# Gathering the selector matmuls of block 0 into two groups of four chunks

## Chip, cores, metric

The kernel runs on one core of a Trainium2 chip. The metric is the device time of one execution in microseconds (us). "Before" is the kernel as it was, "after" the changed one. Times were taken in rounds, several executions of each kernel on the same chip.

## The reference, cut to what matters

Two pairs of layers work on 2048 tokens of width 1024: LayerNorm and a dilated sliding-window attention (32 heads of 32, window 8, step 2), then LayerNorm and a gated feed-forward layer.

```python
def _A_ref(x, wqkv, wo):                       # attention, cut
    q, k, v = ...                              # x @ wqkv, split by heads
    off = jnp.arange(W) * dil                  # W, dil = 8, 2
    logits = jnp.einsum("bhsd,bhswd->bhsw", q, kg) * scale
    logits = jnp.where(mask[None, None, :, :], logits, -1e9)
    attn = _softmax(logits, axis=-1)
    o = jnp.einsum("bhsw,bhswd->bhsd", attn, vg)
    return o.transpose(...).reshape(B, S, D) @ wo
x = x + _A_ref(_layernorm(x), A_wqkv, A_wo)
x = x + _B_ref(_layernorm(x), B_W_gate, B_W_up, B_W_down)
# ... and the same two lines once more
```

The change touches `logits` for the first block of 512 tokens (block 0) of the first pair.

## The kernel before

The tokens go through in four blocks of 512, twice. For block 0 the scores are made in eight chunks c = 0 to 7. TensorE makes q_c and k_c (eight 128x512 matmuls each, called an acc group here), ScalarE casts each out of PSUM, and VectorE multiplies q_c with the eight shifted views of k_c into prod_c (128 partitions x 4096). A selector matmul then sums over the partitions that belong to one head. Its weights are only 128x32, so four stand side by side in the array, one for each quarter of the tokens. Each chunk needs eight of them.

```python
    def red_mm(n, prod, first, last):
        ...
        with pe_group():                 # keeps TensorE in this order
            for wh in range(2):
                for tq in range(TPB):
                    mm(st["L"][32 * tq:32 * tq + 32, WH * wh:WH * (wh + 1), :], lhsT=sel[:],
                       rhs=prod[:, WH * wh:WH * (wh + 1), tq * P:(tq + 1) * P],
                       start=first, stop=last, skip_group_check=True, tile_position=(0, 32 * tq))

    def prod_direct_steps(n):            # block 0 only
        prods = {}
        def mult(c):
            def f():
                prods[c] = work.tile([P, W, BLK], BF16, tag="t", name=f"prod_{c}")
                ...
        def red(c):
            def f():
                red_mm(n, prods.pop(c), c == 0, c == KC - 1)
            return f
        return [mult(c) for c in range(KC)], [red(c) for c in range(KC)]
```

The program is written as a list of events with a time each (in estimated us). They are sorted and emitted, and so the order of the instructions on each engine comes out of these numbers (`t_qk0` and `t_qk1` are where the q and k work of blocks 0 and 1 begins, `GRP` is 1.73, the time of one acc group):

```python
    GAP0 = 2.05
    ...
    spread(qk_steps(0, ln_a[0], "qk01"), t_qk0, GAP0)     # q_0 k_0 q_1 k_1 ... k_7
    mults, reds = prod_direct_steps(0)
    for c in range(KC):
        ev.append((t_qk0 + GAP0 * (2 * c + 2.0), mults[c]))
        if c < KC - 2:
            ev.append((t_qk0 + GAP0 * (2 * c + 4.5), reds[c]))
    ...
    ev.append((t_qk1 + 0.5 * GRP, reds[KC - 2]))
    ev.append((t_qk1 + 2.5 * GRP, reds[KC - 1]))
    ev.append((t_qk1 + 2.6 * GRP, lambda: softmax(0)))
    ln1(2, t_qk0 + 10.0, t_qk1 + 5.0, True, 4.5)          # LayerNorm of block 2, on ScalarE
    spread(qk_steps(1, ln_a[1], "qk01"), t_qk1, GRP)      # q_0 q_1 q_2 k_0 ... of block 1
```

`ln1` gives ScalarE two statistics passes for each of four tiles of 128 tokens, and later one apply for each; at the time in its third argument a DMA transposes the result.

## Time and profile before

| | before |
|---|---|
| time, median of 3 (range) | 1630.64 us (1630.27 to 1630.65) |
| TensorE busy | 1618.6 of 1628.4 us |
| chain of waits, share of TensorE | 95% |
| TensorE waiting for other engines | 3.3 us |
| stretch, first acc_q matmul of block 0 to first acc_k of block 1 | 63.04 - 24.69 = 38.35 us |

The stretch holds everything that the change touches on TensorE.

From the profile page of before, the span, the first line of busy times (us, share of the span, instructions) and the chain of waits by engine:

```profile
span 1628.4 us, 18703 instructions
...
PE 1618.6 (99%) x7589; PEld 782.2 (48%) x7638; DVE 1062.6 (65%) x926; ACT 506.1 (31%) x1050; POOL 255.7 (16%) x220
...
PE 95%; DVE 4%; issue 1%; DMA 0%; POOL 0%; DVEq 0%
```

From the waits view of before, for TensorE: waiting line, releaser, us in total, times, longest.

```profile
PE scratch L129 <- DVE ones L296: 1.5, 1, 1.5
PE dacc L129 <- DVE x L700: 0.8, 1, 0.8
PE acc_v L129 <- DVE xnT_first L103: 0.6, 1, 0.6
PE tp L364 <- DVE xn_first L103: 0.4, 1, 0.4
```

TensorE is fed nearly all the time. VectorE's 65% is of no use as a limit here: only what makes the stream of TensorE shorter, or tears a hole into it, moves the time.

The timeline of before, for TensorE, around one selector group and around the last two (start us, length, engine and line, operation, shapes, count):

```profile
31.60 1.89 PE L129 MATMUL acc_q<-xnT_first,w_qk_q 128*128 128x512 bf16 x8
33.42 0.61 PE L129 MATMUL L<-prod,sel 128*32 128x512 bf16 x8
33.96 1.95 PE L129 MATMUL acc_k<-xnT_first,w_qk_k 128*128 128x512 bf16 x8
35.75 1.89 PE L129 MATMUL acc_q<-xnT_first,w_qk_q 128*128 128x512 bf16 x8
...
58.34 0.62 PE L129 MATMUL L<-prod,sel 128*32 128x512 bf16 x8
58.88 3.67 PE L129 MATMUL acc_q<-xnT_a,w_qk_q 128*128 128x512 bf16 x16
62.49 0.62 PE L129 MATMUL L<-prod,sel 128*32 128x512 bf16 x8
63.04 1.95 PE L129 MATMUL acc_k<-xnT_a,w_qk_k 128*128 128x512 bf16 x8
```

Go by the starts: matmuls are pipelined and their ends are modelled, so lengths overlap. From 31.60 to 35.75 are 4.15 us; two acc groups without selectors between take 2 x 1.73 = 3.45. One selector group so costs 0.70 us. In the start of each single matmul, the eight stand as two sets of four, 0.216 us apart, which is 0.43 us of work. The other 0.27 us lie at the borders: 0.310 us instead of 0.216 on entry, 0.312 on exit, 0.271 before the second matmul after it (0.25 together; the last 0.02 are the 0.01 by which the fourth of a set starts behind the first, twice). A border between two acc groups, where weights and output tile change too, costs nothing (0.216 us again, from 35.530 to 35.746).

The same stretch of before, for the last two products (on the right, in brackets, the engine's idle time before it and its releaser):

```profile
53.80 2.31 DVE L103 TENSOR_TENSOR prod<-q,k 128x4096 bf16<-128x4096 bf16 x1 [2.41 <-ACT k L480]
56.72 0.58 ACT L480 CAST k<-acc_k 128x512 bf16<-128x512 f32 x1 [0.87 <-PE acc_k L129]
57.39 2.31 DVE L103 TENSOR_TENSOR prod<-q,k 128x4096 bf16<-128x4096 bf16 x1 [1.27 <-ACT k L480]
```

prod_7 ends at 59.7 and is used at 62.49. That is 2.8 us of slack.

### The profile page before, as it was taken

To read this page: it belongs to the slowest core of one execution; us is meant where nothing else is said; L and a number is where in the kernel's file an instruction comes from. 1 tells how busy PE (TensorE), PEld (TensorE's weight loads), DVE (VectorE), ACT (ScalarE), POOL (GpSimd) and SP (SyncE) were. 2 spreads that over 40 slices of the span, in tenths; PEclk is the share of its full clock that TensorE was granted. 3 is DMA by queue.
4 is the path that set the end of the run, shared out by engine and by line. 5 is a ranking of instruction groups with operands and counts; after the bars stand their busy time and mean duration, and the time that the engine had idled before them with its cause. 6 is when DMAs were issued, how large, how long until landed. Compare 5 with 4: busy or idle time off the path is not lost.

```text
span 1628.4 us, 18703 instructions
## 1 busy us (share of the span) xinstructions
PE 1618.6 (99%) x7589; PEld 782.2 (48%) x7638; DVE 1062.6 (65%) x926; ACT 506.1 (31%) x1050; POOL 255.7 (16%) x220
## 2 busy tenths in 40 slices
PE   9999999999999999999999999999999999999999
PEld 6644445444544445444454444544445444444444
DVE  5799899985497927949179492894818958211211
ACT  4754313243241513405134051331513311131110
POOL 2421003310250102201052010520105100000000
PEclk9999999999999999999999999999999999999999
DMA  9579656746476485664857647577484764655451
GB/s 303 93 203 252 167 177 199 192 156 200 136 215 175 155 233 171 184 175 150 229 181 185 187 150 225 162 203 212 151 231 154 194 205 155 206 164 172 156 168 65
DMA packets 371463, 296.83 MB, mean 182 GB/s; under 512 B 142512, under 2 KB 351664, under 8 KB 370480
## 3 DMA queue, kind: packets, MB, share of 16 engines
q1 hardware_dynamic: 371088, 295.23, 63.2%
q8 instruction: 60, 0.98, 0.3%
q10 hardware_dynamic: 288, 0.39, 0.1%
q14 instruction: 27, 0.22, 0.0%
HBM read 256.77 MB, written 21.00 MB: 171 GB/s over the span
## 4 chain that ended last, share of the span: by engine, by line
PE 95%; DVE 4%; issue 1%; DMA 0%; POOL 0%; DVEq 0%
PE acc_g L129 24%; PE acc_u L129 24%; PE dacc L129 22%; PE acc_v L129 7%; PE acc_k L129 6%; PE acc_q L129 6%; PE acc_wo L129 6%; DVE t L541 2%; DVE ac L551 1%; PE L L129 1%; DVE pv L603 0%; DVE x L648 0%; DVE pv L604 0%; DVE ac L541 0%; DMA x<-in_A_x_dram 0%
## 5 line engine op out<-in xcount | busy, mean ns | idle before, releaser
L129 PE MATMUL acc_g<-xnT_b,w_g 128*128 128x512 bf16 x1792 | 423.4, 379 | 0.0
L129 PE MATMUL acc_u<-xnT_b,w_u 128*128 128x512 bf16 x1792 | 423.3, 379 | 0.0
L129 PE MATMUL dacc<-w_d,hT 128*128 128x512 bf16 x1759 | 386.5, 379 | 2.5 <-DVE x L700 0.8
L672 ACT ACTIVATE r<-acc_g 128x512 bf16<-128x512 f32 x224 | 133.4, 596 | 747.1 <-PE acc_g L129 746.0
L673 DVE TENSOR_TENSOR hT<-acc_u,r 128x512 bf16<-128x512 f32 x224 | 153.7, 687 | 315.1 <-PE acc_u L129 313.5
L129 PEld LDWEIGHTS <-hT 128*128 128x128 bf16 x1792 | 175.4, 98 | 212.3 <-issue 1.0
L129 PEld LDWEIGHTS <-w_g 128*128 128x128 bf16 x1792 | 174.8, 98 | 212.7 <-issue 3.0
L129 PEld LDWEIGHTS <-w_u 128*128 128x128 bf16 x1792 | 175.4, 98 | 211.4
L541 DVE TENSOR_TENSOR t<-q,k 128x2048 f32<-128x2048 bf16 x84 | 191.7, 2290 | 8.6 <-ACT k L480 5.8
L551 DVE TENSOR_TENSOR ac<-ac,t 128x2048 f32<-128x2048 f32 x84 | 191.7, 2282 | 0.4
L485 POOL COPY kh<-k 128x14 bf16<-128x14 bf16 x64 | 81.2, 1273 | 471.9 <-ACT k L480 471.8
L700 DVE TENSOR_TENSOR x<-dacc,x 128x512 bf16<-128x512 f32 x64 | 42.5, 687 | 164.0 <-PE dacc L129 164.0
L603 DVE TENSOR_TENSOR pv<-a,vhm 128x4096 bf16<-128x4096 bf16 x64 | 145.2, 2282 | 0.0
L129 PE MATMUL acc_wo<-w_o,oT 128*128 128x512 bf16 x496 | 111.0, 379 | 0.8
L245 POOL TENSOR_TENSOR st_b<-st_b,neg_half 128x1 f32<-128x1 f32 x29 | 56.4, 1956 | 288.6 <-ACT st_b L244 288.6
L245 POOL TENSOR_TENSOR st_a<-st_a,neg_half 128x1 f32<-128x1 f32 x32 | 41.9, 1315 | 319.2 <-ACT st_a L244 319.1
L484 POOL COPY k<-kh 128x14 bf16<-128x14 bf16 x48 | 70.5, 1469 | 65.9 <-DVE t L541 43.8
L129 PEld LDWEIGHTS <-oT 128*128 128x128 bf16 x512 | 50.0, 98 | 60.4
L604 DVE TENSOR_TENSOR pv<-pv 128x2048 bf16<-128x2048 bf16 x64 | 77.4, 1215 | 0.2
L476 ACT CAST q<-acc_q 128x512 bf16<-128x512 f32 x64 | 37.3, 583 | 73.2 <-PE acc_q L129 73.2
L240 ACT ACTIVATE xn_b<-x 128x1024 bf16<-128x1024 bf16 x29 | 30.3, 1045 | 89.3 <-DVE x L648 89.3
L480 ACT CAST k<-acc_k 128x512 bf16<-128x512 f32 x64 | 37.3, 583 | 63.0 <-PE acc_k L129 62.8
(131 smaller groups left out, 1209.1 us busy)
## 6 DMA issues: line engine op xcount, KB each, us to landing
w_g<-in_B_W_gate_dram SPq DMA_DIRECT2D x56, 1024.0 KB, 7.0
w_u<-in_B_W_up_dram SPq DMA_DIRECT2D x56, 1024.0 KB, 5.4
w_d<-in_B_W_down_dram SPq DMA_DIRECT2D x48, 1024.0 KB, 5.8
w_o<-in_A_wo_dram SPq DMA_DIRECT2D x16, 1024.0 KB, 7.2
vhm<-v_d SPq DMA_DIRECT2D x32, 284.0 KB, 6.9
v_d<-vT SPq DMA_DIRECT2D x8, 1024.0 KB, 10.0
oT<-o_d SPq DMA_DIRECT2D x32, 256.0 KB, 4.4
w_d<-in_B_W_down_dram SPq DMA_DIRECT2D x16, 512.0 KB, 4.0
```

Source lines behind the costliest of these rows:

```text
L129: tail_pe[0] = nc.tensor.matmul(*args, **kwargs).ins
L245: nc.gpsimd.tensor_tensor(rstd, vpe, neg_half[:, 0:1], op=ALU.pow)
L476: tail_act[0] = nc.scalar.copy(q[:], acc[:]).ins
L484: nc.gpsimd.tensor_copy(k[:, 0:HALO], khalo[n - 1][:, c, :])
L485: nc.gpsimd.tensor_copy(khalo[n][:, c, :], k[:, BLK:BLK + HALO])
L541: nc.vector.tensor_tensor(t[:], i0, i1, op=ALU.mult)
L551: nc.vector.tensor_tensor(o, ac[:], t[:], op=ALU.add)
L603: nc.vector.tensor_tensor(tt[:], a_bc, v_sh, op=ALU.mult)
L604: nc.vector.tensor_tensor(tt[:, 0:4], tt[:, 0:4], tt[:, 4:8], op=ALU.add)
L672: tail_act[0] = nc.scalar.activation(r[:], acc[:], ACT.Relu).ins
L673: nc.vector.tensor_tensor(hold["hT"][:, j, :], accs["u"][:], r[:], op=ALU.mult)
L700: nc.vector.tensor_tensor(xs, ac[t], xs, op=ALU.add)
```

## The change

Its intent is to have fewer of the 0.27 us borders: two groups of 32 selector matmuls for eight of 8. The products of a group must then live until the group runs, so six of the eight go to the big buffers. The spacing of the events is tightened to fit, and the transpose for block 2 moves back.

```diff
-                prods[c] = work.tile([P, W, BLK], BF16, tag="t", name=f"prod_{c}")
+                if c in (3, 4):
+                    prods[c] = work.tile([P, W, BLK], BF16, tag="t", name=f"prod_{c}")
+                else:
+                    prods[c] = big_tile([P, W, BLK], f"prod_{c}")
...
-        def red(c):
-            def f():
-                red_mm(n, prods.pop(c), c == 0, c == KC - 1)
+        def red(c0, c1):
+            def f():
+                for c in range(c0, c1):
+                    red_mm(n, prods.pop(c), c == 0, c == KC - 1)
...
-        return [mult(c) for c in range(KC)], [red(c) for c in range(KC)]
+        return [mult(c) for c in range(KC)], [red(0, KC // 2), red(KC // 2, KC)]
...
-    GAP0 = 2.05
+    GAP0 = 1.9
...
-        if c < KC - 2:
-            ev.append((t_qk0 + GAP0 * (2 * c + 4.5), reds[c]))
+    ev.append((t_qk0 + GAP0 * 9.5, reds[0]))
...
-    ev.append((t_qk1 + 0.5 * GRP, reds[KC - 2]))
-    ev.append((t_qk1 + 2.5 * GRP, reds[KC - 1]))
-    ev.append((t_qk1 + 2.6 * GRP, lambda: softmax(0)))
-    ln1(2, t_qk0 + 10.0, t_qk1 + 5.0, True, 4.5)
+    ev.append((t_qk1 + 0.5 * GRP, reds[1]))
+    ev.append((t_qk1 + 0.6 * GRP, lambda: softmax(0)))
+    ln1(2, t_qk0 + 10.0, t_qk1 + 7.5, True, 4.5)
```

## The prediction

> What bounds the kernel now. The profile page has TensorE busy 1618.6 of 1628.4 us at a granted clock of 1.0; the chain of waits is 95% TensorE; in the waits view TensorE waits 3.3 us for other engines in the whole program. So the time is the length of the TensorE stream, and only time taken out of it, or a new hole in it, counts.
>
> What the change touches. The first ~65 us. All 64 selector matmuls (128x32 weights, four column tiles side by side) remain; on TensorE only their place differs: eight groups of 8 become two of 32, one after k_4 of block 0, one after the first q of block 1.
>
> Gain. A group of 8 costs 0.70 us: two acc_q groups with a selector group and an acc_k between start 4.15 us apart (31.60 to 35.75), without it 3.45. Inside, four matmuls start 3 ns apart and the next four 0.216 us later, so pure work is 0.43 us; entry (0.310 instead of 0.216), exit (0.312) and the second matmul after it (0.271) make up 0.27. The Trainium skill, TensorEngine Tiling (Array Packing), Key Properties, says that a change of tiling mode drains the engine; these gaps agree. A group of 32 should take 8 x 0.216 + 0.25 = 1.97 us. Estimate: 8 x 0.70 - 2 x 1.97 = 1.6 us less stream, the most the change can win, 0.1%.
>
> What may eat it. TensorE reaches both groups earlier, relative to the products.
> Group 1 (there at about 42.0 us): prod_3 is bound by VectorE, which runs without a gap from 29.5 us in the timeline of before, prod_3 at 40.72 to 43.01. The matmuls of prods 0 to 2 last until 43.3: no wait, 0.3 us to spare.
> Group 2 (there at about 56.1 us; before, the last single group at 62.5) needs k_7's cast on ScalarE, then prod_7 (2.3 us). ScalarE runs in order (the skill, TensorE: Matmul & The Clock Gate, calls its queue strict FIFO), and in the new order k_6's cast stands behind two LayerNorm statistics passes and one apply of block 2. With pitches from the trace (cast 0.46, statistics 1.18 and 1.06, apply 1.13) and ScalarE idle 43.6 to 45.9 waiting for q_5 behind group 1, I get k_6 cast at 54.4, k_7 at 56.0; prod_6 54.4 to 56.7, prod_7 56.7 to 59.0. TensorE wants prod_7 at 57.4: a new hole of about 1.6 us (0.5 to 2.5). Estimate, not seen.
>
> So gain and hole nearly cancel. The third acc group after it (k_0 of block 1, 63.04 in before) should start at 62 to 63.5.
>
> Afterwards. Softmax of block 0 starts about 59.6 instead of 63.2, and VectorE's chain, full from 70 to 130 us, ends 2 to 3 us earlier; but TensorE did not wait for it (0.1 us idle around acc_wo), so this wins at most 0.1. From 140 us on the order of TensorE is the same, full clock, no waits: same time.
>
> Predicted time: 1630.3 us (before 1630.64), 8 in 10 between 1629.0 and 1631.9. Chances: faster by over 2%: 0.003; within 2%: 0.994; slower by over 2%: 0.003.
>
> Right if: two selector groups of about 2.0 us (the second 3 to 4 because of a hole); the waits view showing a new wait of the L matmuls on a product of 1 to 2 us at 57 to 59 us, none at 42 to 44; k_6's cast about 3 us after its accumulation; softmax 3 to 4 us earlier; stage borders after 70 us within 1 us of before.
> Wrong if: the hole is absent (then 1629.0); or a late x load or a GpSimd power holds the statistics on ScalarE and so k_6 and k_7 (then 1632 or more); or the switch cost doesn't shrink with grouping; or products in big buffers wait for a buffer.

## The result

| | before | after |
|---|---|---|
| time, median of 4 (range) | 1630.45 us (1630.27 to 1630.65) | 1630.16 us (1629.99 to 1630.61) |
| ratio, 95% interval | | 0.9999 (0.9981 to 1.0016) |
| stretch | 38.35 us | 63.16 - 24.82 = 38.34 us |

A ratio is the mean time of one kernel's fast runs over that of the other's fast runs of the same rounds, so it is not quite the ratio of the medians quoted. The result is "same", as predicted (1630.3).

The page of after, the same lines:

```profile
span 1628.4 us, 18703 instructions
...
PE 1616.3 (99%) x7589; PEld 783.2 (48%) x7638; DVE 1063.0 (65%) x926; ACT 505.5 (31%) x1050; POOL 258.0 (16%) x220
...
PE 94%; DVE 4%; issue 1%; ACT 1%; DMA 0%; POOL 0%; DVEq 0%
```

TensorE is busy 2.3 us less in the same span, and ScalarE appears in the chain. The waits view of after for TensorE says where:

```profile
PE scratch L129 <- DVE ones L296: 1.5, 1, 1.5
PE L L129 <- DVE prod L103: 1.4, 1, 1.4
PE tp L364 <- DVE xn_first L103: 1.3, 2, 0.9
```

The second line is new: one wait of a selector matmul for a product. (The third belongs to the start of the run; it differs from run to run.) The timeline of after for TensorE shows both groups:

```profile
40.36 1.89 PE L129 MATMUL acc_k<-xnT_first,w_qk_k 128*128 128x512 bf16 x8
42.18 1.91 PE L129 MATMUL L<-prod,sel 128*32 128x512 bf16 x32
44.02 1.95 PE L129 MATMUL acc_q<-xnT_first,w_qk_q 128*128 128x512 bf16 x8
...
54.44 1.89 PE L129 MATMUL acc_q<-xnT_a,w_qk_q 128*128 128x512 bf16 x8
56.26 1.48 PE L129 MATMUL L<-prod,sel 128*32 128x512 bf16 x24
59.10 0.61 PE L129 MATMUL L<-prod,sel 128*32 128x512 bf16 x8 [1.36 <-DVE prod L103]
59.65 3.67 PE L129 MATMUL acc_q<-xnT_a,w_qk_q 128*128 128x512 bf16 x16
63.16 1.89 PE L129 MATMUL acc_k<-xnT_a,w_qk_k 128*128 128x512 bf16 x8
```

The first group runs through in 1.84 us (42.18 to 44.02). The second stops after 24 matmuls, until prod_7 comes at 59.05. By starts the hole is larger than the 1.36 in brackets: the last of the 24 started at 57.36, so the next was due at 57.57 and came 1.53 us late. The acc_k of block 1 then starts where it would have in before.

The reason stands on ScalarE and VectorE. The timeline of after, with the lines that matter:

```profile
49.26 1.89 PE L129 MATMUL acc_k<-xnT_first,w_qk_k 128*128 128x512 bf16 x8
...
50.30 1.04 ACT L240 ACTIVATE xn_a<-x 128x1024 bf16<-128x1024 bf16 x1
...
51.52 1.04 ACT L241 ACTIVATE xn_a<-x 128x1024 bf16<-128x1024 bf16 x1
...
52.56 1.23 ACT L263 ACTIVATE xn_a<-x,st_a 128x1024 bf16<-128x1024 bf16 x1
...
53.88 0.56 ACT L480 CAST k<-acc_k 128x512 bf16<-128x512 f32 x1
...
54.55 4.50 DVE L103 TENSOR_TENSOR prod<-q,k 128x4096 bf16<-128x4096 bf16 x2 [2.85 <-ACT k L480]
...
55.40 0.57 ACT L480 CAST k<-acc_k 128x512 bf16<-128x512 f32 x1
```

k_6's accumulation was ready for its cast at about 51.2 us: its acc group starts at 49.26, and a cast that waits for nothing else starts 1.93 us after its group (31.60 to 33.52 in before). The cast starts at 53.88, because two statistics passes and an apply of block 2 (L240, L241, L263) stand ahead of it in ScalarE's order. VectorE waits 2.85 us for it, then makes prod_6 and prod_7 without a gap, until 59.05. In before the same three passes stood ahead of k_6 (its cast was at 53.15), but there TensorE wanted prod_7 only at 62.49.

So far this is a reading of one trace. Whether the saving is real, and whether ScalarE's queue ate it, is for the experiments.

### The profile page after: what moved, and what is told of

Read it like the earlier page. It is cut to its first block, busy times and chain, and to the rows that moved or that the text cites. A ratio compares the mean times of both kernels' runs of the same rounds, so it can differ in the third digit from the quotient of the medians.

```text
span 1628.4 us, 18703 instructions
## 1 busy us (share of the span) xinstructions
PE 1616.3 (99%) x7589; PEld 783.2 (48%) x7638; DVE 1063.0 (65%) x926; ACT 505.5 (31%) x1050; POOL 258.0 (16%) x220
## 4 chain that ended last, share of the span: by engine, by line
PE 94%; DVE 4%; issue 1%; ACT 1%; DMA 0%; POOL 0%; DVEq 0%
PE acc_g L129 24%; PE acc_u L129 24%; PE dacc L129 22%; PE acc_v L129 7%; PE acc_wo L129 6%; PE acc_q L129 6%; PE acc_k L129 6%; DVE t L545 2%; DVE ac L555 1%; PE L L129 0%; DVE pv L607 0%; DVE x L652 0%; DVE prod L103 0%; DVE pv L608 0%; DVE ac L545 0%
## 5 line engine op out<-in xcount | busy, mean ns | idle before, releaser
L240 ACT ACTIVATE xn_b<-x 128x1024 bf16<-128x1024 bf16 x29 | 30.3, 1045 | 90.2 <-DVE x L652 90.2
```

## The experiments

All twelve runs were timed in five rounds, each against before on its own chip. They came in three batches on three chips; the medians of before in them were 1630.30 (after_again, late1, lngap, pairs), 1630.17 (early1, lngap2, kcast, gap205) and 1630.48 us (halves, bufs, late2, lngap3). Before itself had executions up to 1632.93. The "wait" is that of the selector matmuls for a product, from the waits view.

| run | what is different | selector groups | stretch us | wait us | median us (range) | ratio (95%) |
|---|---|---|---|---|---|---|
| after_again | the change once more | 2 | 38.34 | 1.4 | 1630.24 (1630.15 to 1630.70) | 0.9998 (0.9985 to 1.001) |
| late1 | second group one acc group later | 2 | 36.80 | 0 | 1628.57 (1628.46 to 1628.90) | 0.9988 (0.9974 to 1.0002) |
| lngap | LayerNorm of block 2 spread wider, wrong result | 2 | 36.90 | 0 | 1628.62 (1628.52 to 1629.60) | 0.9989 (0.9976 to 1.0001) |
| pairs | before, groups of two chunks | 4 | 37.28 | 0 | 1629.48 (1629.10 to 1630.23) | 0.9993 (0.9981 to 1.0006) |
| early1 | second group one acc group earlier | 2 | 41.55 | 2.9 | 1633.30 (1631.78 to 1633.64) | 1.0018 (1.0005 to 1.0031) |
| lngap2 | lngap made correct | 2 | 36.90 | 0 | 1629.42 (1629.06 to 1631.23) | 0.9997 (0.9985 to 1.001) |
| kcast | casts of k_6, k_7 on VectorE | 2 | 37.05 | 0 | 1628.83 (1628.72 to 1629.22) | 0.9992 (0.998 to 1.0005) |
| gap205 | spacing back to 2.05 | 2 | 37.18 | 0.2 | 1629.01 (1628.80 to 1630.39) | 0.9995 (0.9981 to 1.0009) |
| halves | before, groups cut in half | 15 | 40.22 | 0 | 1631.99 (1631.75 to 1632.13) | 1.0009 (0.9997 to 1.0022) |
| bufs | before, with buffers and spacing of the change | 8 | 38.35 | 0 | 1630.60 (1630.44 to 1631.01) | 1.0001 (0.9988 to 1.0015) |
| late2 | second group two acc groups later | 2 | 36.73 | 0 | 1629.17 (1628.73 to 1631.69) | 0.9994 (0.9982 to 1.0007) |
| lngap3 | lngap2, transpose later still | 2 | 36.90 | 0 | 1628.87 (1628.46 to 1630.64) | 0.9993 (0.9981 to 1.0006) |

The intervals of the ratios are wider than the effects: alone they separate only early1 from before. I therefore read the stretch, which repeats to 0.01 us (38.34 in both traces of the change, 38.35 in before and in bufs), and use the times as a check.

### The change again

No edit; it is there to be compared with its variants in the same rounds.

> The changed kernel once more, to be timed in the same rounds as its variants. The stretch from the first acc_q matmul of block 0 to the first acc_k matmul of block 1 was 38.35 us in before and 38.34 us in after. All theories: again within 0.4 us of before, one wait of 1.2 to 1.7 us before the matmuls of prod_7, stretch 38.3 us.

Measured as expected: stretch 38.34, wait 1.4 us, 0.06 us from the median of before.

### late1: take the hole away by coming later

```diff
-    ev.append((t_qk1 + 0.5 * GRP, reds[1]))
-    ev.append((t_qk1 + 0.6 * GRP, lambda: softmax(0)))
+    ev.append((t_qk1 + 1.5 * GRP, reds[1]))
+    ev.append((t_qk1 + 1.6 * GRP, lambda: softmax(0)))
```

> The second group of 32 selector matmuls stands one acc_q group (1.73 us) later. Theory (grouping saves 6 x 0.27 = 1.6 us and the wait for prod_7 ate it): TensorE reaches prod_7 at about 59.3 us, prod_7 is ready at 59.1, so no wait; stretch 36.8 us, time 1628.6 us. Rival 1 (grouping saves nothing, the entry and exit cost is per selector matmul): no wait, but stretch 38.3 us and time as before, 1630.4. Rival 2 (the saving is real, but is given back after 65 us, where acc_wo waits for the attention output): stretch 36.8, but a new wait before acc_wo and time 1630.2.

The timeline of late1 for TensorE:

```profile
54.34 3.62 PE L129 MATMUL acc_q<-xnT_a,w_qk_q 128*128 128x512 bf16 x16
57.89 1.91 PE L129 MATMUL L<-prod,sel 128*32 128x512 bf16 x32
59.73 1.95 PE L129 MATMUL acc_q<-xnT_a,w_qk_q 128*128 128x512 bf16 x8
```

The second group now runs through in 1.84 us, like the first. Stretch 36.80 and time 1628.57, both as the theory said. All five times lie below all five of the change in the same rounds (at most 1628.90 against at least 1630.15). Both rivals fall: grouping does save, and the saving arrives at the end. From the first acc_k of block 1 to the first acc_wo it is 50.07 us in late1 and after.

### pairs, halves: is the cost per group?

```diff
@@ pairs, on before
+        def red(c0, c1): ...                    # as in the change
+        return [...], [red(c, c + 2) for c in range(0, KC, 2)]
+        if c in (1, 3, 5): ev.append((t_qk0 + GAP0 * (2 * c + 4.5), reds[c // 2]))
+    ev.append((t_qk1 + 2.5 * GRP, reds[3]))
@@ halves, on before
+    def red_mm(n, prod, first, last, whs=(0, 1)):
+            for wh in whs:
+        return [...], [red(c, h) for c in range(KC) for h in range(2)]
+            ev.append((t_qk0 + GAP0 * (2 * c + 4.5), reds[2 * c]))
+            ev.append((t_qk0 + GAP0 * (2 * c + 5.5), reds[2 * c + 1]))
```

Both have the buffers of the change. The last groups of halves stand before the first q of block 1 and behind each of its first three.

> Before with four groups of 16 selector matmuls instead of eight of 8, buffers as in the change, spacing as in before. Theory (0.27 us per group): four groups fewer save 1.1 us, no waits, stretch 37.3, time 1629.4. Rival 1 (cost per matmul): stretch 38.35, time 1630.4.

> Before, each group of 8 selector matmuls cut into two groups of 4 with an acc group between (one pair stands together: 15 groups in all), buffers as in the change. Same matmuls, 7 more entries and exits. Theory (0.27 us per group): stretch 38.35 + 7 x 0.27 = 40.2 us, time 1632.1. Rival (cost per matmul): stretch 38.35, time 1630.2.

With the same 64 matmuls, the stretch is 40.22, 38.35, 37.28 and 36.80 us for 15, 8, 4 and 2 groups. Per group that is 0.27 (1.87 over 7), 0.27 (1.07 over 4) and 0.24 us (0.48 over 2). The last is too small by the mark: where the last group stands right ahead of acc_k, as in the first three, 0.06 us of its exit (0.271 instead of 0.216 before the second matmul) falls behind the end of the stretch, and in late1 it does not. late2 below has its last group there and a stretch of 36.73, so 0.27 again (0.55 over 2). The cost goes with the number of groups, not of matmuls. The times follow, 1631.99, 1630.2 to 1630.5, 1629.48 and 1628.57.

### bufs: buffers and spacing alone

```diff
@@ on before
-    GAP0 = 2.05
+    GAP0 = 1.9
+    # prods 3 and 4 in work buffers, the rest in big ones; transpose at t_qk1 + 7.5
```

> Before with the change's buffers, spacing of 1.9 and later transpose, but the eight single groups. Theory (those parts alone win nothing where eight groups leave no wait): stretch 38.35, no new wait, time 1630.2. Rival (the big buffers or the spacing are a gain or a loss of their own): more than 0.3 us away.

The stretch is the same, 38.35. The time, 1630.60, is 0.1 above before in these rounds, but 0.4 above what was expected, and so outside the 0.3 that the expectation allowed; before itself was 0.3 slower in this batch than in the one ahead of it. In its trace the first acc_wo waits 0.2 us for the attention output from DRAM, and the part from acc_k to acc_wo is 50.52 us instead of 50.13, so a small loss there is possible. The buffers alone win nothing.

### early1: make the hole larger

```diff
+        # mults[7] a little sooner, so that it still stands ahead
-    ev.append((t_qk1 + 0.5 * GRP, reds[1]))
-    ev.append((t_qk1 + 0.6 * GRP, lambda: softmax(0)))
+    ev.append((t_qk1 - 0.1, reds[1]))
+    ev.append((t_qk1 - 0.05, lambda: softmax(0)))
```

> The second group of 32 stands one acc_q group earlier than in the change, straight behind k_7. Theory (prod_7's time is set by ScalarE's queue and VectorE, so every step that the group stands earlier is added to the wait): prod_7 ready at about 59.1 as before, wait 1.73 us longer (about 3.1 us in the waits view), stretch from the first acc_q of block 0 to the first acc_k of block 1 about 40.0 us, time 1631.9 us, so slower than both kernels. Rival (position doesn't matter, TensorE only makes up the order): stretch 38.3, time 1630.2.

A miss, in an instructive way. The wait was 2.9 us, near the 3.1 expected, but the stretch became 41.55 instead of 40.0, and four of five times lay at 1633.1 to 1633.6. The timeline of early1 for TensorE, and then the windows view (busy time of each engine in us with its instructions, then the granted clock, then the DMA share):

```profile
54.76 1.05 PE L129 MATMUL L<-prod,sel 128*32 128x512 bf16 x16
57.13 0.61 PE L129 MATMUL L<-prod,sel 128*32 128x512 bf16 x8 [1.32 <-DVE prod L103]
59.33 1.04 PE L129 MATMUL L<-prod,sel 128*32 128x512 bf16 x8 [1.59 <-DVE prod L103]
60.31 6.45 PE L129 MATMUL acc_q<-xnT_a,w_qk_q 128*128 128x512 bf16 x24
```

```profile
54.00:57.00 3.00, 1.81 (x20) 0.72 (x19) 2.22 (x2) 3.00 (x10) 1.58 (x2) 1.00 0.04 3
57.00:60.00 3.00, 1.28 (x16) 0.35 (x15) 2.28 (x2) 0.34 (x1) 2.60 (x4) 0.85 0.01 3
60.00:63.00 3.00, 3.00 (x12) 1.25 (x9) 2.51 (x3) 0.00 (x0) 0.00 (x0) 0.58 0.03 5
63.00:66.00 3.00, 3.00 (x16) 1.99 (x15) 1.29 (x2) 2.44 (x5) 0.00 (x0) 1.00 0.00 0
```

prod_7 ended as long after the start of the stretch as in after (34.23 us in both), so the wait is the predicted one. But before it was over, the granted clock (the share of TensorE's full clock that the trace records as let through) had fallen. The 0.85 and 0.58 come to half the clock for 3.4 us, from about 59.1 to 62.5, and the acc_q matmuls start 0.427 us apart instead of 0.216 until then. That is the further 1.5 us.

Of the other four executions there is no trace. A drop of 3.4 us takes the mean clock to 0.999, so the one at 1631.78, with 1.0, had none, and its time is what the theory had said (1631.9). That the other three slow ones had it I take from their times. Their mean clock of 0.999 does not show it by itself: the profiled execution of after has 0.999 too, from a fall behind its last matmul (0.66 in the windows view, from 1626.0 us to the end).

The Trainium skill, "TensorE: Matmul & The Clock Gate", What's actually happening, says that the clock is halved after an idle window of about 3.4 us, and that the window runs free of the kernel. The halved rate agrees. The window here was not all idle: in the 3.4 us before the drop (55.70 to 59.11) TensorE was busy for 0.72 us, above all with the eight matmuls at 57.13. That the drop was absent once in five would fit a free-running window, but no run shows that this is why. In after, with its single hole of 1.5 us, the matmuls behind it start 0.216 us apart as usual.

### lngap, lngap2, lngap3 and gap205: take the hole away on ScalarE

Here the second group stays where the change put it. In the first three the LayerNorm of block 2 is spread wider, so k_6 and k_7 are cast sooner. In gap205 only the spacing goes back, which puts a statistics pass into a time when ScalarE idled (2.29 us before q_5's cast in after).

```diff
-    ln1(2, t_qk0 + 10.0, t_qk1 + 7.5, True, 4.5)
+    ln1(2, t_qk0 + 10.0, t_qk1 + 7.5, True, 6.5)     # lngap
+    ln1(2, t_qk0 + 10.0, t_qk1 + 20.0, True, 6.5)    # lngap2
+    ln1(2, t_qk0 + 10.0, t_qk1 + 33.0, True, 6.5)    # lngap3
@@ gap205
-    GAP0 = 1.9
+    GAP0 = 2.05
```

> The second group stays where the change put it; the LayerNorm statistics of block 2 on ScalarE are spread wider (6.5 instead of 4.5 units apart), which puts one statistics pass and the apply that stood before k_6's cast behind k_7's cast. Theory (the wait comes from ScalarE's queue): k_6's cast at about 52.1, k_7's at 54.7, prod_7 done at 57.6 instead of 59.1, so a wait of at most 0.2 us, stretch 36.9, time 1628.7. Rival (VectorE or GpSimd bounds prod_7, not ScalarE): wait stays above 1 us, time 1630.2.

> The run lngap again, with the transpose of block 2's LayerNorm put after its last apply (lngap issued it before and so gave wrong numbers). Theory: as lngap, now correct: no wait above 0.2 us at the second group, stretch 36.9, time 1628.6. Rival (lngap won because it skipped the wait of the transpose for the applies): the wait or a new one comes back, time 1630.2.

> lngap2 with the transpose of block 2's LayerNorm still later in the DMA queue, behind the weight load of the v projection that it held up in lngap2 (issued at 84.9 instead of 79.8 us, and TensorE waited 0.5 us for it). Theory: that wait is gone, stretch 36.9, from there to the first acc_wo 50.1 instead of 50.7 us, time 1628.6. Rival (the v weights were late for another reason): 50.7 again, 1629.4.

> The change with its spacing put back to 2.05. The order on TensorE stays; on ScalarE one LayerNorm statistics pass now stands before q_5's cast, where ScalarE idled 2.3 us. Theory: k_6's cast at about 52.6, k_7's at 55.2, prod_7 done at 58.1 (all after the first acc_q start at 24.8), a wait of 0.4 to 0.8 us, stretch 37.4, time 1629.2: between the change and the version without a wait. Rival (the spacing has no part in it): wait 1.4 us, time 1630.2.

lngap had a relative error of 0.27: I had left the transpose ahead of the last two applies, so it read old data. Its timing still says what was asked: k_6's cast started at 52.17, k_7's at 54.63, prod_7 ended at 57.60, no wait, stretch 36.90. From the timeline of lngap:

```profile
52.17 0.57 ACT L480 CAST k<-acc_k 128x512 bf16<-128x512 f32 x1
...
55.31 2.29 DVE L103 TENSOR_TENSOR prod<-q,k 128x4096 bf16<-128x4096 bf16 x1 [0.16 <-ACT k L480]
...
56.25 2.02 PE L129 MATMUL L<-prod,sel 128*32 128x512 bf16 x32
```

lngap2, the correct form, has the same stretch, 36.90, but its time was 1629.42 instead of 1628.6. Something took part of the gain back further on. Its timeline for the DMA queue of SyncE and for TensorE:

```profile
78.97 5.23 SPq L118 DMA_TRANSPOSE xnT_a<-xn_a  x1
84.30 0.52 SPq L118 DMA_DIRECT2D o_d<-ohm  x1
84.93 0.39 SPq L118 DMA_DIRECT2D w_v<-in_A_wqkv_dram  x1
...
91.47 0.82 PE L129 MATMUL acc_v<-xnT_a,w_v 128*128 128x512 bf16 x3 [0.50 <-DMA w_v<-in_A_wqkv_dram]
```

The transpose waited at the head of that queue for the last apply, and behind it the load of the v weights, which went out at 84.93 (79.76 in after). TensorE then waited for them. In lngap3 the transpose stands behind the load. The load went out at 78.56, the wait was gone, and the part to acc_wo was 50.07 again, as the theory expected. Three of its times are 1628.46 to 1628.87. Two are at 1630.5 and 1630.6; in the profiled one of them the stretch is still 36.90, and the end of the run is longer: from the start of the last matmul to the end 5.83 us instead of 4.28 in before. The four writes of the result, the last work of the run, took a median of 2.8 us to land there instead of 2.0. Why is open; nothing that the edit touches lies there.

gap205 came out between the two, as expected, somewhat better (wait 0.2 instead of 0.4 to 0.8, stretch 37.18 instead of 37.4).

### kcast: take the two casts out of ScalarE's queue

```diff
+                    if n == 0 and c >= 6:
+                        dv(nc.vector.tensor_copy, k[:, HALO:HALO + BLK], acc[:])
+                    else:
                         tail_act[0] = nc.scalar.copy(k[:, HALO:HALO + BLK], acc[:]).ins
```

> The casts of k_6 and k_7 of block 0 go to VectorE, in front of their products; ScalarE keeps its order otherwise. Theory (these two casts wait in ScalarE's queue): k_6 cast on VectorE at about 51.7, prod_6 52.5 to 54.8, k_7 cast 54.8, prod_7 55.5 to 57.8; wait at the second group 0.1 to 0.4 us, stretch 37.0, time 1628.9, though VectorE has 1.4 us more to do. Rival (VectorE's own time for the products is the limit): with more work on VectorE the wait grows to over 2 us, time 1631.

VectorE got 1.4 us more to do (two casts of 0.68 us) on the way to prod_7, and yet the hole went: k_6 cast at 51.46, prod_7 done at 57.59. Stretch 37.05, time 1628.83, as the theory said. The waits view lists no wait, but the second group takes 2.10 us from start to start instead of 1.84, so some 0.26 us were still lost in it (timeline of kcast):

```profile
51.46 0.68 DVE L103 CAST k<-acc_k 128x512 bf16<-128x512 f32 x1
...
56.10 2.17 PE L129 MATMUL L<-prod,sel 128*32 128x512 bf16 x32
```

VectorE's own work was not what held prod_7; the wait for ScalarE was.

### late2: still later

```diff
-    ev.append((t_qk1 + 0.5 * GRP, reds[1]))
+    ev.append((t_qk1 + 2.5 * GRP, reds[1]))
```

The softmax moves with it, as in late1.

> The second group two acc_q groups later than in the change. Theory: the wait was already gone at one, so nothing more is won: stretch 36.8, time 1628.6, as late1. Rival (some of the wait was left in late1): under 1628.3.

Nothing more was won: the stretch is 36.73 (the group now stands right ahead of acc_k, so 0.06 us of its exit falls behind the mark). The median, 1629.17, is 0.6 above late1's; in the trace acc_k to acc_wo is 50.17 instead of 50.07, of which 0.06 is that exit. One execution was at 1631.69. The spread I can't place. late1 is the version to take: correct, and in its rounds 1.7 us below both kernels.

## Why the prediction was right

It said 1630.3 us; measured were 1630.16 and, again, 1630.24. That the mechanism was right is shown below. That the time came out so close is in part luck: a hole of 0.5 to 2.5 us had been allowed for, and the 0.3 us between the two medians is not in the traces, where from the first acc_q of block 0 to the first acc_wo it is 88.41 us instead of 88.48.

- The gain. Predicted 1.6 us less stream, from 0.27 us per group. Shown by late1 without a hole: from the first acc_q of block 0 to the first acc_wo 86.87 us instead of 88.48, so 1.61 (1.55 in the stretch, the rest is the exit behind its mark). By starts the groups of 32 took 1.84 us, plus 0.06 before the second matmul after them and 0.09 on entry, so 1.99; predicted 1.97.
- Group 1 without a wait: right (42.18 to 44.02 without a gap), with prod_3 done at 43.07.
- The hole. Predicted 1.6 us at 57.4, because k_6 would be cast by 54.4, k_7 by 56.0 and prod_7 end at 59.0. Measured: 54.4, 56.0 and 59.05, a hole of 1.53 by starts (1.36 in the waits view). That ScalarE's queue makes it is shown by lngap and its two correct forms, where only the LayerNorm of block 2 stands elsewhere in the order and the hole is gone, by kcast, which takes the two casts out of the queue and leaves some 0.26 us of it although VectorE has more to do, and by early1, where the wait grows with the group's earlier place.
- Cancelling. Predicted 62 to 63.5 for acc_k of block 1, measured 63.16.
- Afterwards. Softmax started at 59.77 (predicted 59.6). VectorE was 2.4 us earlier at the first product with v (68.9 instead of 71.3), and TensorE gained nothing from it: from acc_k to acc_wo 50.07 instead of 50.13 us, and the 0.06 is the exit of before's last group.
- What it did not see. It listed a late load and a GpSimd power as dangers; neither came. It did not name the real danger of a larger hole, the halved clock of early1. After's hole did not bring it.

The Trainium skill, "TensorEngine Tiling (Array Packing)", Key Properties, says that a change of tiling mode drains TensorE. The border cost per group agrees with it; that draining is the mechanism, no run shows. That ScalarE's queue is strictly first in, first out ("TensorE: Matmul & The Clock Gate", Architectural detail) agrees with after: the cast of k_6, ready at 51.2, started at 53.88.

## What to carry to other kernels

When you gather work to save borders, what the gathered work needs becomes due all at once and, because the stream has become shorter, sooner; look at the order on the engines that make it before you choose the place. A hole as large as the gain looks in the total just like a change without effect, so measure the stretch that you changed and its waits, not only the time. If the saving is there and a wait ate it, moving the group by one step can bring it back, and in this case moving it the other way cost more than the wait itself, since the clock fell.

## What the Trainium skill lacked or had wrong

- "TensorEngine Tiling (Array Packing)", Key Properties, gives no cost for changing the tiling mode. Here one group of four-column-tile matmuls between 128x128 matmuls cost 0.27 us on top of its work, alike for groups of 4, 8, 16 and 32 matmuls.
- "TensorE: Matmul & The Clock Gate", HAM oscillation, states the rule as no idle gaps over about 3.4 us, and the section after it tells of frequent short ones without a number. In early1 two holes of 1.32 and 1.59 us (waits view), with eight matmuls between them, came with a halved rate (0.427 instead of 0.216 us per matmul). In the 3.41 us before the drop TensorE was busy for 0.72 us. A single hole of 1.36 us did not do it in the two traces of after (busy for 2.04 of 3.41 us around it in the first). Idle time close together may count together; only one trace shows the drop.
- No page that I read says how much the waits view understates a hole in TensorE's stream. "Perfetto Trace Analysis", Tensor Engine Instruction, says that ends of matmuls are estimated; here the difference was 0.17 us (1.36 in the view, 1.53 by starts).
